# Weight conversions of the first layer issued later and in another order, a third pair of part buffers, earlier normalizations, and SBUF addresses moved by 32 bytes

## The chip, the core and the metric

The kernel runs on one core of a Trainium2 chip. The metric is the device time of one execution in microseconds (us). TensorE (PE) multiplies, VectorE (DVE) and ScalarE (ACT) do the elementwise work, SyncE (SP) and GpSimd (POOL) issue the transfers. Each engine runs its own instructions in order and waits on semaphores for the others.

## What is computed

Eight batches of eight heads attend to keys and values that are first averaged over groups of 8 rows; the result goes through two feed-forward layers of 512 to 2048 to 512.

```python
k_p = k.reshape(B, H, Sp, 8, D).mean(axis=3); v_p = v.reshape(B, H, Sp, 8, D).mean(axis=3)
scores = 1 / np.sqrt(D) * np.matmul(q, k_p.transpose(0, 1, 3, 2))
attn = softmax(scores); x = np.matmul(attn, v_p)      # 4608 tokens x 512
h = np.maximum(x @ w_in, 0.0);  x = h * h @ w_out      # layer 1, weights given as float64
h = x @ w2_in;  out = np.maximum(0.01 * h, h) @ w2_out # layer 2
```

## The kernel before

The 4608 tokens are nine blocks of 512. Float32 values are split into a high and a low part, so each product is three passes of 128x512 matmuls. A chunk is 128 of the 2048 hidden columns; there are 16, and a weight tile holds two of them.

**Weight conversion.** The weights of layer 1 arrive as pairs of 32-bit words and are converted in 16 tiles: numbers 0 to 7 are input weights, 8 to 15 output weights. `weight_steps` names the steps by letters: a is `exponent` on ACT (L231); b is `first_bits`, two DVE instructions (L235, L238); c is `low_term`, two DVE instructions (L249, L252); d is the sum on DVE (L293) and, in the same step, the copy of the high part on ACT (L296); e is the low part on DVE (L300), which reads that copy.

**First products of blocks 0 and 1** (`first_products`). The list `ORDER` has 32 units, each one call of `first`: 12 matmuls of one chunk (L872) into one of three accumulator banks, then `relu` on ACT (L882), then a store of the result to DRAM by POOL. Units 0 to 11 also carry the attention of block 1 (`second_attention`). A bank is used again three units later, after the relu that empties it. `conversion(u)` issues the weight steps of unit u; the table `begins` says at which unit tile n begins. In the unit of `begins` come a of the next tile and c, d of this one; in the unit behind it come b of the next tile and then e of this one. Tile 5 holds chunks 10 and 11 of block 0 (units 10 and 11), tile 6 chunks 12 and 13 (units 16 and 17), tile 7 chunks 14 and 15 (units 18 and 19).

**Second products of blocks 0 and 1** (`second_products`). 32 units again, one call of `second` each: 12 matmuls (L911). A unit first squares a stored result on ACT (L885) and splits the next one into `gh` and `gl` on DVE (`in_parts`, L890, L891; two buffers of each). Behind the matmuls come attention steps of block 2 (`Steps.upto`) and one step of the conversion of layer 2's weights (`w2.tick`). At the end of a block `finish` empties four banks, two on ACT (L927) and two on DVE (L925).

**The rest.** Blocks 2 to 8 run both products chunk by chunk with the next block's attention between; layer 2 follows, with 7 forms of a 2x2 scheme on 384 columns (L1299) and 512-column products (L1366). All orders are written out in Python; no scheduler moves anything.

**Addresses.** Pools on the left and the right side of SBUF hold all tiles. Before, a tile of 32 bytes (`pad`) stands at the end of the right side, and the tiles of attention and layer 1 and all weights begin at multiples of 64 bytes; the forms of layer 2 (`fh`, `fl`, `t1`, `t2`, `sums`) begin 32 bytes past one, by the tile `off`.

Of the kernel before, what the change touches and what calls it, by code (L numbers as in the profile page):

```python
# [16 lines left out]
P = 128  # L17
# [5 lines left out]

C_ID, C_PAR, C_VM, C_RA, C_RB, C_RP, C_N = 0, 128, 138, 140, 141, 142, 144

# [18 lines left out]
def attention_relu2_leaky_kernel(  # L44
# [36 lines left out]
    common = ctx.enter_context(tc.tile_pool(name="sb", bufs=1, side="left"))  # L81
    pad = ctx.enter_context(tc.tile_pool(name="pad", bufs=1, side="right"))
    nc.gpsimd.memset(pad.tile([P, 8], F32, tag="pad", name="pad"), 0.0)
    weights = ctx.enter_context(tc.tile_pool(name="wt", bufs=1, side="right"))
# [6 lines left out]
    BUFS = {"raw": 3, "val": 3, "qt": 2, "r": 3, "gh": 2, "gl": 2, "s": 2, "kt": 2, "kp": 2}  # L91
    BUFS.update({"m": 4, "l": 4, "st": 3, "val": 2})

# [24 lines left out]

    cst = sb([P, C_N], F32, "cst")
    ident = cst[:, C_ID : C_ID + P]  # L120
# [152 lines left out]
    def weight_steps(w, kind, i):  # L273


        st = {}

        def load_words():
            t = sb([P, 1024, 2], U32, weight_tag(kind, i))
            src, to = words_of(w, kind, i)  # L280
            nc.sync.dma_start(out=to(t), in_=src)
            st["low"], st["top"] = t[:, :, 0], t[:, :, 1]

        def bits():
            val = st["val"] = sb([P, 1024], U32, "val")
            first_bits(val, st["top"])

        def term():
            low_term(st["val"], st["top"], st["low"])

        def high():
            w = st["w"] = f32(st["val"])
            nc.vector.tensor_tensor(out=w, in0=w, in1=f32(st["low"]), op=ALU.add)  # L293
            t = st["parts"] = sb([P, 2, 1024], F32R, weight_tag(kind, i))
            place(kind, i, t)
            nc.scalar.copy(t[:, 0], w)  # L296

        def low():
            t = st["parts"]
            nc.vector.tensor_tensor(out=t[:, 1], in0=st["w"], in1=f32(t[:, 0]), op=ALU.subtract)  # L300

        return load_words, lambda: exponent(st["top"]), bits, term, high, low

    class Weights:
# [8 lines left out]
        def do(self, what, n):  # L313

            if n < len(self.steps):
                for x in what:
                    self.steps[n][" abcde".index(x)]()

# [106 lines left out]
    def k_mask(b):  # L425

        full, tail = KEYS // P, KEYS % P
        kp = kps.pop(b)
        km = (home() if b == 0 else sb([P, 512], F32, "r"))[:, : full * 2 * D]
        km = km.rearrange("p (c j d) -> p c j d", j=2, d=D)  # L430
        kt = sb([P, 2, D], F32, "km")
        par = cst[:, C_PAR : C_PAR + 2 * NK].rearrange("p (c j) -> p c j", j=2)
        for out, c0, c1, n in ((km, 0, full, P), (kt.unsqueeze(1), full, NK, tail)):
            shape = [n, c1 - c0, 2, D]
            nc.vector.tensor_tensor(
                out=out[:n],
                in0=kp[:n, c0:c1, :].unsqueeze(2).to_broadcast(shape),
                in1=par[:n, c0:c1, :].unsqueeze(3).to_broadcast(shape),
                op=ALU.mult,
            )  # L440
        kms[b] = km, kt
# [285 lines left out]
    def start():  # L727

        t0, rest = 0, {}
        for word in START:  # L730
# [18 lines left out]
            elif x in "abcde":  # L749
                w1.do(x, n)  # L750
            elif x == "k":
# [115 lines left out]
    def first(blk, c, at=None):  # L867
        hi, lo = xsplit[blk]
        ps = bank() if at is None else acc_bank(at % (KC - 1))
        for kc in range(KC):  # L870
# [15 lines left out]

    def in_parts(r):
        gh = sb([P, T], F32R, "gh")
        gl = sb([P, T], F32R, "gl")
        nc.vector.tensor_copy(gh, r)  # L890
        nc.vector.tensor_tensor(out=gl, in0=r, in1=f32(gh), op=ALU.subtract)  # L891
        return gh, gl
# [39 lines left out]
    class Steps:  # L932
# [8 lines left out]
        def upto(self, n):  # L941
            kind = "scores"
            while self.done < n:
                kind, step = self.steps[self.done]
                step()
                self.done += 1
            if kind != "scores" and self.done < len(self) and self.steps[self.done][0] == "normalize":
                self.steps[self.done][1]()
                self.done += 1
# [91 lines left out]

    begins = {2 * n - 2 if n < FC // 2 else FC - 2 + (n - FC // 2) * 5 // 2: n for n in range(1, FC - 1)}

    def conversion(u):
        if u in begins:
            n = begins[u]
            if n + 1 < FC - 1:
                w1.do("a", n + 1)
            w1.do("bcd" if n == 1 else "cd", n)
        elif u - 1 in begins:  # L1050
            n = begins[u - 1]
            if n + 1 < FC - 1:
                w1.do("b", n + 1)
            w1.do("e", n)

# [33 lines left out]
    def second_products():  # L1089
# [4 lines left out]
        for u in range(n_units):  # L1094
# [6 lines left out]
            if u + 1 < n_units:  # L1101
                g_next = in_parts(mids.pop(u + 1))
            if u >= n_units - 2:
                turn.pop(0)()
            second(c, acc, g)
            if 4 <= u < 9:
                w1.do("abcde"[u - 4], FC - 1)
            steps.upto(min(len(steps) * u // (n_units - 3), len(steps)))
            if u >= FC // 2:
                w2.tick()  # L1110
            if c == FC - 1:
# [366 lines left out]
```

## Time and profile before

| | us |
|---|---|
| median of 3 runs | 1737.35 |
| lowest, highest | 1734.87, 1738.37 |
| the profiled execution | 1736.26 |
| its span, first to last instruction | 1734.4 |
| PE busy in the span | 1693.5 |
| first products of blocks 0 and 1, from unit 0 | 47.1 to 170.6 |
| second products of blocks 0 and 1 | 170.6 to 280.9 |

The profiled execution lies 1.1 us under the median. Its span is 1.9 us shorter than its own time. The busy time of PE counts pipelined matmuls, so it does not tell the pace; the starts of neighbouring matmuls do.

### The profile page before, as it was taken

To read this page: it belongs to the slowest core of one execution; us is meant where nothing else is said; L and a number is where in the kernel's file an instruction comes from. 1 tells how busy PE (TensorE), PEld (TensorE's weight loads), DVE (VectorE), ACT (ScalarE), POOL (GpSimd) and SP (SyncE) were. 2 spreads that over 40 slices of the span, in tenths; PEclk is the share of its full clock that TensorE was granted. 3 is DMA by queue.
4 is the path that set the end of the run, shared out by engine and by line. 5 is a ranking of instruction groups with operands and counts; after the bars stand their busy time and mean duration, and the time that the engine had idled before them with its cause. 6 is when DMAs were issued, how large, how long until landed. Compare 5 with 4: busy or idle time off the path is not lost.

```text
span 1734.4 us, 21693 instructions
## 1 busy us (share of the span) xinstructions
PE 1693.5 (98%) x8312; PEld 1460.2 (84%) x8312; DVE 1110.3 (64%) x2020; ACT 627.1 (36%) x1496; POOL 19.1 (1%) x39
## 2 busy tenths in 40 slices
PE   6889999999999999999999999999999999999999
PEld 5768778888888888888888899999999999999997
DVE  7888777666666667565435555565566675666564
ACT  4555244344343443434333322332332332223221
POOL 0012000000000000000000000000000000000000
PEclk9999999999999999999999999999999999999999
DMA  8924552323222332231004202201202411320220
GB/s 229 338 72 145 174 182 89 92 92 95 88 95 88 104 104 73 95 112 61 13 25 162 81 1 73 74 12 61 74 25 98 170 48 62 110 103 13 104 74 37
DMA packets 106296, 162.44 MB, mean 94 GB/s; under 512 B 44112, under 2 KB 44240, under 8 KB 105168
## 3 DMA queue, kind: packets, MB, share of 16 engines
q1 hardware_dynamic: 103632, 152.67, 26.4%
q0 software_dynamic: 2560, 8.39, 1.3%
q8 instruction: 65, 1.06, 0.3%
q14 instruction: 39, 0.32, 0.1%
HBM read 111.75 MB, written 49.28 MB: 93 GB/s over the span
## 4 chain that ended last, share of the span: by engine, by line
PE 91%; DVE 6%; ACT 2%; issue 1%; DMA 0%; SPq 0%; DVEq 0%; ACTq 0%
PE acc L911 20%; PE ps L1299 20%; PE ps L872 18%; PE acc L1366 15%; PE ps L1366 8%; PE acc L872 4%; PE ps L587 2%; PE ps L650 1%; PE ps L551 1%; PE ps L702 0%; ACT s L608 0%; PE ps L701 0%; PE ps L704 0%; PE ps L703 0%; DVE xl L679 0%
## 5 line engine op out<-in xcount | busy, mean ns | idle before, releaser
L911 PE MATMUL acc<-gh,wo 128*128 128x512 f32 x1152 | 296.4, 395 | 4.0 <-DVE gh L890 1.9
L872 PE MATMUL ps<-xh,wi 128*128 128x512 f32 x896 | 297.0, 394 | 0.0
L1299 PE MATMUL ps<-fh,wi 128*128 128x384 f32 x1344 | 289.2, 337 | 0.1
L1299 PEld LDWEIGHTS ps<-fh,wi 128*128 128x128 f32 x1344 | 243.1, 188 | 22.1 <-DVE gh L1312 0.4
L911 PEld LDWEIGHTS acc<-gh,wo 128*128 128x128 f32 x1152 | 213.1, 188 | 51.1 <-DVE gh L890 4.5
L1366 PE MATMUL acc<-wo,sh 128*128 128x512 f32 x768 | 205.6, 390 | 0.0
L872 PEld LDWEIGHTS ps<-xh,wi 128*128 128x128 f32 x896 | 168.2, 188 | 35.0 <-issue 0.2
L872 PE MATMUL ps<-xl,wi 128*128 128x512 f32 x448 | 174.5, 389 | 0.0
L1299 PE MATMUL ps<-fl,wi 128*128 128x384 f32 x672 | 171.2, 336 | 0.0
L890 DVE CAST gh<-r 128x512 fp32r<-128x512 f32 x112 | 47.7, 425 | 187.0 <-ACT r L885 186.7
L911 PE MATMUL acc<-gl,wo 128*128 128x512 f32 x576 | 159.6, 391 | 0.0
L1366 PEld LDWEIGHTS acc<-wo,sh 128*128 128x128 f32 x768 | 141.5, 188 | 15.6
L882 ACT ACTIVATE r<-ps 128x512 f32<-128x512 f32 x112 | 67.7, 605 | 212.0 <-PE ps L872 212.0
L911 PEld LDWEIGHTS acc<-gl,wo 128*128 128x128 f32 x576 | 108.7, 189 | 23.4
L1299 PEld LDWEIGHTS ps<-fl,wi 128*128 128x128 f32 x672 | 121.4, 188 | 0.0
L1366 PE MATMUL acc<-wo,sl 128*128 128x512 f32 x384 | 120.2, 392 | 0.0
L608 ACT ACTIVATE s<-ps,m 128x72 f32<-128x72 f32 x240 | 72.3, 331 | 105.9 <-DVE m L599 105.9
L1312 DVE TENSOR_TENSOR u<-gh,ps 128x384 f32<-128x384 f32 x48 | 26.6, 554 | 120.0 <-PE ps L1299 120.0
L1366 PE MATMUL ps<-wo,sh 128*128 128x512 f32 x384 | 102.8, 389 | 0.0
L872 PEld LDWEIGHTS ps<-xl,wi 128*128 128x128 f32 x448 | 84.2, 188 | 16.6
L1366 PEld LDWEIGHTS acc<-wo,sl 128*128 128x128 f32 x384 | 72.1, 188 | 18.3 <-DVE sl L1347 3.7
L891 DVE TENSOR_TENSOR gl<-r,gh 128x512 fp32r<-128x512 f32 x112 | 77.6, 692 | 8.0 <-DVE gh L890 0.9
(206 smaller groups left out, 2362.2 us busy)
## 6 DMA issues: line engine op xcount, KB each, us to landing
wi<-in_moe_w_in SPq DMA_DIRECT2D x8, 1024.0 KB
wo<-in_moe_w_out SPq DMA_DIRECT2D x8, 1024.0 KB
val<-in_moe_w_in SPq DMA_DIRECT2D x16, 512.0 KB
val<-in_moe_w_out SPq DMA_DIRECT2D x16, 512.0 KB
w2p<-val SPq DMA_DIRECT2D x16, 512.0 KB
wo<-w2p SPq DMA_DIRECT2D x8, 1024.0 KB
xh<-x SPq DMA_DIRECT2D x10, 768.0 KB
xl<-x SPq DMA_DIRECT2D x10, 768.0 KB
```

Of the source, the lines that this page charges most:

```text
L551: nc.tensor.transpose(ps[:, cc * P : (cc + 1) * P], raw[:, cc * P : (cc + 1) * P], ident)
L587: nc.tensor.matmul(ps[: r0 + n, c2 * PAIR : (c2 + 1) * PAIR], lhsT=qt[:, cc, : r0 + n], rhs=kts[b][:, keys], start=True, stop=True,)
L608: nc.scalar.activation(out=s[:, g, :], in_=ps[:, h * SP : (h + 1) * SP], func=AF.Exp, bias=m[:, g : g + 1], accum_out=None if i in early e ...
L650: nc.tensor.transpose(ps[:, cc * P : (cc + 1) * P], flat[:, cc * PAIR : cc * PAIR + P], ident)
L872: nc.tensor.matmul(ps, lhsT=w[:, kc], rhs=x[kc], start=(kc == 0 and n == 0), stop=(kc == KC - 1 and n == 2),)
L882: nc.scalar.activation(out=r, in_=ps, func=AF.Relu)
L890: nc.vector.tensor_copy(gh, r)
L891: nc.vector.tensor_tensor(out=gl, in0=r, in1=f32(gh), op=ALU.subtract)
L911: nc.tensor.matmul(acc[m], lhsT=w[:, m * P : (m + 1) * P], rhs=x, start=(c == 0 and n == 0), stop=(c == FC - 1 and n == 2),)
L1299: nc.tensor.matmul(at, lhsT=w[:, FORMS[j], kc], rhs=x[j][:, kc], start=m == 0 and j in (0, 1, 4), stop=m == 5, skip_group_check=True,)
L1312: nc.vector.tensor_tensor(out=out_, in0=x, in1=at, op=ALU.add)
L1366: nc.tensor.matmul(self.acc[i], lhsT=x[g % 2][c][t][:, at], rhs=self.outs[p][:, part_, c], start=p == 0 and m == 0, stop=p == PAIRS - 1 an ...
```

## The change

Five things are done. The ACT copy of the high part becomes a step of its own, D; it still directly follows d, except for tile 1, where it moves to the next unit. In the second unit of a tile, e now stands ahead of b of the next tile. Tiles from number 6 on begin at unit 2n + 1 (13, 15, ... 29) where tile 6 began at 10, tile 7 at 12, tile 8 at 14 and the later ones about every 2.5 units up to 29; a and b of tile 6 stand in unit 12. The accumulator of unit u is bank (u + 2) mod 3 and not u mod 3. In the second products every third pair of parts goes into two `st` buffers; the last two units of block 0 carry no attention steps and no tick; and a normalization may be taken ahead of one pooling step. All tiles move by 32 bytes, except the identity, the pooled keys `kt`, and the small `m` and `l`, which stay at multiples of 64; the forms of layer 2 come to multiples of 64.

```diff
-C_ID, C_PAR, C_VM, C_RA, C_RB, C_RP, C_N = 0, 128, 138, 140, 141, 142, 144
+C_ID, C_PAR, C_VM, C_RA, C_RB, C_RP, C_N = 16, 0, 10, 12, 13, 14, 144
...
-    pad = ctx.enter_context(tc.tile_pool(name="pad", bufs=1, side="right"))
-    nc.gpsimd.memset(pad.tile([P, 8], F32, tag="pad", name="pad"), 0.0)
...
-    BUFS.update({"m": 4, "l": 4, "st": 3, "val": 2})
+    BUFS.update({"m": 4, "l": 3, "st": 3, "val": 2})
...
-    cst = sb([P, C_N], F32, "cst")
+    cst = sb([P, C_N + 8], F32, "cst")[:, :C_N]
...
             place(kind, i, t)
-            nc.scalar.copy(t[:, 0], w)
+
+        def high_copy():
+            nc.scalar.copy(st["parts"][:, 0], st["w"])
...
-        kt = sb([P, 2, D], F32, "km")
+        kt = sb([P, 2 * D + 8], F32, "km")[:, : 2 * D].rearrange("p (j d) -> p j d", j=2)
...
-        ps = bank() if at is None else acc_bank(at % (KC - 1))
+        ps = bank() if at is None else acc_bank((at + 2) % (KC - 1))
...
-    def in_parts(r):
-        gh = sb([P, T], F32R, "gh")
-        gl = sb([P, T], F32R, "gl")
+    def in_parts(r, tags=("gh", "gl")):
+        gh, gl = (sb([P, T], F32R, tag) for tag in tags)
...
         def upto(self, n):
-            kind = "scores"
+            kind = ""
...
-            if kind != "scores" and self.done < len(self) and self.steps[self.done][0] == "normalize":
-                self.steps[self.done][1]()
+            near = "".join(k[:1] or "-" for k, _ in self.steps[self.done : self.done + 2])
+            if kind != "scores" and near.lstrip("-")[:1] == "n":
+                step = self.steps.pop(self.done + near.index("n"))
+                self.steps.insert(self.done, step)
+                step[1]()
...
-    begins = {2 * n - 2 if n < FC // 2 else FC - 2 + (n - FC // 2) * 5 // 2: n for n in range(1, FC - 1)}
+    LATE = 6
+    begins = {2 * n - 2 if n < LATE else 2 * n + 1: n for n in range(1, FC - 1)}
...
-            if n + 1 < FC - 1:
+            if n + 1 < FC - 1 and n + 1 != LATE:
                 w1.do("a", n + 1)
-            w1.do("bcd" if n == 1 else "cd", n)
+            w1.do("bcd" if n == 1 else "cdD", n)
...
-            if n + 1 < FC - 1:
+            w1.do("De" if n == 1 else "e", n)
+            if n + 1 < FC - 1 and n + 1 != LATE:
                 w1.do("b", n + 1)
-            w1.do("e", n)
+        elif u == 2 * LATE:
+            w1.do("ab", LATE)
...
-                g_next = in_parts(mids.pop(u + 1))
+                apart = (u + 1) % 3 == 2 and u + 3 < n_units
+                g_next = in_parts(mids.pop(u + 1), ("st", "st") if apart else ("gh", "gl"))
...
-            steps.upto(min(len(steps) * u // (n_units - 3), len(steps)))
-            if u >= FC // 2:
-                w2.tick()
+            if c < FC - 2 or blk:
+                steps.upto(min(len(steps) * u // (n_units - 3), len(steps)))
+                if u >= FC // 2:
+                    w2.tick()
```

On DVE, behind unit 11, the conversions stand back to back. Before, from b of tile 7 on (`wi_719` is tile 7 as loaded, `wi_983` the parts of tile 6, `wo_852` tile 8, `wi_1057` the parts of tile 7):

```order
L235 TENSOR_SCALAR val<-wi_719 128x1024 [waits DMAHW7_49]
L238 SCALAR_TENSOR_TENSOR val<-wi_719,val 128x1024 [waits DVE_49]
L300 TENSOR_TENSOR wi_983<-val,wi_983 128x1024
L249 TENSOR_SCALAR wi_719<-val 128x1024 [waits DVE_49]
L252 SCALAR_TENSOR_TENSOR wi_719<-wi_719 128x1024 [waits DVE_49]
L293 TENSOR_TENSOR val<-val,wi_719 128x1024 [waits DVE_49]
L235 TENSOR_SCALAR val<-wo_852 128x1024 [waits DMAHW0_49,Activation_49]
L238 SCALAR_TENSOR_TENSOR val<-wo_852,val 128x1024 [waits DVE_49]
L300 TENSOR_TENSOR wi_1057<-val,wi_1057 128x1024 [waits Activation_49]
```

Now, at the same place (`wi_611` is tile 6 as loaded, `wi_1058` its parts, `wi_714` tile 7, `wi_1102` its parts):

```order
L233 TENSOR_SCALAR val<-wi_611 128x1024 [waits DMAHW6_49,Activation_49]
L236 SCALAR_TENSOR_TENSOR val<-wi_611,val 128x1024 [waits DVE_49]
L247 TENSOR_SCALAR wi_611<-val 128x1024 [waits DVE_49]
L250 SCALAR_TENSOR_TENSOR wi_611<-wi_611 128x1024 [waits DVE_49]
L291 TENSOR_TENSOR val<-val,wi_611 128x1024 [waits DVE_49]
L300 TENSOR_TENSOR wi_1058<-val,wi_1058 128x1024 [waits Activation_49]
L233 TENSOR_SCALAR val<-wi_714 128x1024 [waits DMAHW7_49]
L236 SCALAR_TENSOR_TENSOR val<-wi_714,val 128x1024 [waits DVE_49]
L247 TENSOR_SCALAR wi_714<-val 128x1024 [waits DVE_49]
L250 SCALAR_TENSOR_TENSOR wi_714<-wi_714 128x1024 [waits DVE_49]
L291 TENSOR_TENSOR val<-val,wi_714 128x1024 [waits DVE_49]
L300 TENSOR_TENSOR wi_1102<-val,wi_1102 128x1024 [waits Activation_49]
```

Tile 6 now stands here whole, and e of a tile (L300) directly follows its d (L291), where b of the next tile stood between.

On ACT at units 11 to 14, now (`acc_1003` is unit 11's accumulator, `acc_1021` unit 12's, `acc_1041` unit 13's, `wi_1058` the parts of tile 6):

```order
L882 ACTIVATE r<-acc_1003 128x512 [waits DMASW0_49,PE_49,Activation_49]
L229 ACTIVATE wi_611<-wi_611 128x1024 [waits DMAHW6_49]
L882 ACTIVATE r<-acc_1021 128x512 [waits DMASW1_49,PE_49,Activation_49]
L229 ACTIVATE wi_714<-wi_714 128x1024 [waits DMAHW7_49]
L296 CAST wi_1058<-val 128x1024 [waits DVE_49]
L882 ACTIVATE r<-acc_1041 128x512 [waits DMASW2_49,PE_49,Activation_49]
L882 ACTIVATE r<-acc_1065 128x512 [waits DMASW3_49,PE_49,Activation_49]
```

The exponent step of tile 6 (L229) has come from unit 8 to behind the relu of unit 11, and the relu of unit 13 stands behind the copy of tile 6.

On DVE at the end of block 0 in the second products, before, the copies of `finish` (L925) stand behind the steps of a tick (L252, L353):

```order
L252 SCALAR_TENSOR_TENSOR val<-val 128x512
L890 CAST gh<-xh 128x512
L891 TENSOR_TENSOR gl<-xh,gh 128x512
L353 TENSOR_TENSOR r<-r,val 128x512
L925 COPY r<-acc_1456 128x512
L925 COPY r<-acc_1458 128x512
```

On DVE at the same place, now (`acc_1451` and `acc_1453` are banks 1 and 3 of block 0):

```order
L889 CAST gh<-xl 128x512
L890 TENSOR_TENSOR gl<-xl,gh 128x512
L889 CAST gh<-xh 128x512
L890 TENSOR_TENSOR gl<-xh,gh 128x512
L924 COPY r<-acc_1451 128x512
L924 COPY r<-acc_1453 128x512
```

Only parts stand ahead of the copies; the tick and the transposed probabilities have moved behind them.

## Rows read from the trace of the kernel before

**Rows 1.** The page's first part: engine, busy us, share of the span, instructions

```profile
PE 1693.5 (98%) x8312; PEld 1460.2 (84%) x8312; DVE 1110.3 (64%) x2020; ACT 627.1 (36%) x1496; POOL 19.1 (1%) x39
```

**Rows 2.** Waits of PE over the whole span: us in total, times, longest us

```profile
PE acc L872 <- DVE wi L300: 5.0, 2, 4.7
...
PE acc L911 <- DVE gh L890: 1.9, 5, 0.6
...
PE acc L872 <- ACT wi L296: 1.6, 1, 1.6
...
PE acc L911 <- DVE r L925: 1.3, 1, 1.3
```

**Rows 3.** Timeline of PE at unit 10: start us, us, instruction, idle before

```profile
104.42 1.22 PE L872 MATMUL acc<-xh,wi 128*128 128x512 f32 x2 [4.71 <-DVE wi L300]
```

**Rows 4.** Timeline of PE: first matmul of unit 11, of the second products

```profile
113.43 0.39 PE L872 MATMUL acc<-xh,wi 128*128 128x512 f32 x1
...
116.20 0.39 PE L872 MATMUL acc<-wo,wi 128*128 128x512 f32 x1
...
170.60 0.61 PE L911 MATMUL acc<-gh,wo 128*128 128x512 f32 x2
```

**Rows 5.** Timeline of DVE ahead of unit 10's wait

```profile
101.29 0.68 DVE L235 TENSOR_SCALAR val<-wi 128x1024 uint32<-128x1024 uint32 x1
...
103.15 1.22 DVE L300 TENSOR_TENSOR wi<-val,wi 128x1024 fp32r<-128x1024 f32 x1
```

**Rows 6.** Groups of DVE instructions, 44 to 175 us: busy, mean ns, idle before

```profile
L619 DVE TENSOR_REDUCE l<-s 128x8 f32<-128x576 f32 x4 | 3.0, 751 | 1.4 <-ACT s L608 1.4
```

**Rows 7.** Busy us of PE, PEld, DVE, ACT, POOL, clock, DMA, units 11 to 31

```profile
113.40:170.60 57.20, 57.20 (x254) 47.32 (x253) 52.06 (x54) 28.56 (x40) 11.07 (x20) 1.00 0.33 113
```

**Rows 8.** Timeline of DVE: the last conversions ahead of the second products

```profile
157.74 0.68 DVE L235 TENSOR_SCALAR val<-wo 128x1024 uint32<-128x1024 uint32 x1
...
159.60 1.22 DVE L300 TENSOR_TENSOR wo<-val,wo 128x1024 fp32r<-128x1024 f32 x1
160.74 0.69 DVE L249 TENSOR_SCALAR wo<-val 128x1024 uint32<-128x1024 uint32 x1
...
162.72 1.23 DVE L293 TENSOR_TENSOR val<-val,wo 128x1024 f32<-128x1024 f32 x1
165.06 1.22 DVE L300 TENSOR_TENSOR wo<-val,wo 128x1024 fp32r<-128x1024 f32 x1 [1.11 <-ACT wo L296]
```

**Rows 9.** Timeline of ACT: relu of unit 11, an exponent, a copy, three squares

```profile
116.45 0.60 ACT L882 ACTIVATE r<-acc 128x512 f32<-128x512 f32 x1 [2.28 <-PE acc L872]
116.94 1.14 ACT L231 ACTIVATE wo<-wo 128x1024 f32<-128x1024 f32 x1
...
163.98 1.05 ACT L296 CAST wo<-val 128x1024 fp32r<-128x1024 f32 x1 [0.69 <-DVE val L293]
...
168.62 1.66 ACT L885 ACTIVATE xh<-xh 128x512 f32<-128x512 f32 x3
```

**Rows 10.** Busy us of the engines, then the granted clock, around unit 10

```profile
100.50:107.40 6.90, 2.98 (x7) 2.40 (x8) 6.72 (x9) 1.60 (x5) 0.46 (x1) 0.51 0.22 78
```

**Rows 11.** Timeline of PE: units 16 and 17 of the second products

```profile
220.93 0.70 PE L911 MATMUL acc<-gh,wo 128*128 128x512 f32 x2 [0.56 <-ACT xh L885]
222.89 2.50 PE L911 MATMUL acc<-gh,wo 128*128 128x512 f32 x6 [1.25 <-DVE r L925]
...
226.87 2.00 PE L911 MATMUL acc<-gh,wo 128*128 128x512 f32 x8
```

**Rows 12.** Timeline of PE in layer 2

```profile
1204.80 0.51 PE L1299 MATMUL ps<-fl,wi 128*128 128x384 f32 x2
1205.15 1.07 PE L1366 MATMUL ps<-wo,sh 128*128 128x512 f32 x4
```

**Rows 13.** ACT's copies to `fh` (L1206) by source: ns min, median, max

```profile
L1206 ACT CAST fh<-xl x30: 830/833/838, 1030.1 to 1663.1; 128x768 fp32r<-128x768 f32 x30
L1206 ACT CAST fh<-t x22: 821/836/838, 929.8 to 1657.0; 128x768 fp32r<-128x768 f32 x22
```

More of the change, by code (lines that the diff above doesn't have):

```diff
@@ L300, in low @@
             nc.vector.tensor_tensor(out=t[:, 1], in0=st["w"], in1=f32(t[:, 0]), op=ALU.subtract)
-        return load_words, lambda: exponent(st["top"]), bits, term, high, low
+        return load_words, lambda: exponent(st["top"]), bits, term, high, low, high_copy
     class Weights:
@@ L316, in do @@
                 for x in what:
-                    self.steps[n][" abcde".index(x)]()
+                    self.steps[n][" abcdeD".index(x)]()
     class Stored:
@@ L749, in start @@
             elif x in "abcde":
-                w1.do(x, n)
+                w1.do("dD" if x == "d" else x, n)
             elif x == "k":
@@ L1106, in second_products @@
             if 4 <= u < 9:
-                w1.do("abcde"[u - 4], FC - 1)
-            steps.upto(min(len(steps) * u // (n_units - 3), len(steps)))
-            if u >= FC // 2:
-                w2.tick()
+                w1.do(("a", "b", "c", "dD", "e")[u - 4], FC - 1)
+            if c < FC - 2 or blk:
+                steps.upto(min(len(steps) * u // (n_units - 3), len(steps)))
+                if u >= FC // 2:
+                    w2.tick()
             if c == FC - 1:
```

## The prediction

> **What bounds the kernel now.** I read the page's engine shares first: PE is busy for nearly the whole span [rows 1], so a change can only win where PE waits, and loses wherever it makes PE wait. The waits of PE come next [rows 2]: what concerns this change is the low part of an input weight (L300, 5.0 us, one wait of 4.7), its high part (L296, 1.6), the parts of the squares (L890, 1.9) and the copy that empties a bank (L925, 1.3). All lie in the first 281 us. Then I follow three places in the timelines.
>
> The first is unit 10: PE stands 4.71 us for e of tile 5 [rows 3], and DVE comes to that e at 103.15, directly behind b of tile 6 [rows 5].
>
> The second is the stretch from unit 11 to the second products, 113.43 to 170.60 [rows 4]. There PE is the bound: 57.20 of 57.20 us busy [rows 7], and 20 units from 116.20 to 170.60 make 2.72 us a unit [rows 4]. But DVE has little to spare: 52.06 us busy in the same 57.2 [rows 7].
>
> The third is the end of block 0 in the second products, where unit 16's matmuls are stretched by a wait for L925 [rows 2, 11].
>
> **The change, part by part.** The sum is made against the profiled execution, 1736.26 us, which stands 1.1 us under the median of 1737.35.
>
> *Units 0 to 11.* b of tile 6 goes from the DVE path ahead of e of tile 5: 103.15 - 101.29 = 1.86 us [rows 5]. In the units before, e ahead of b lets PE start a unit earlier, and the exponentials with it; DVE waited 1.4 us for these in four normalizations [rows 6], of which I take 1.0, an estimate. The new bank order lets unit 0 start without waiting for the pooled keys, but the units behind it wait for DVE's conversions, so that is in the 1.0 already. Together -2.9 us. The bounds are -1.9 (b alone) and -6.6 (both weight waits of [rows 2], 5.0 + 1.6).
>
> *Units 12 to 31.* Here the change adds a wait, and this is the term that decides. Call X the start of unit 11. The exponent a of tile 6 now stands on ACT behind the relu of unit 11. That relu began 3.02 us behind X and the next ACT instruction 3.51 behind it (116.45 and 116.94 against 113.43 [rows 4, 9]); an exponent takes 1.14 [rows 9]. So b of tile 6 starts on DVE at X + 4.7, and from there DVE has nine whole tiles (6 to 14) ahead of the first pair of parts, and nothing else.
>
> What a tile costs is read at the last tiles of before: b takes 159.60 - 157.74 = 1.86 us, e takes 160.74 - 159.60 = 1.14, c takes 162.72 - 160.74 = 1.98 [rows 8]. From d to e it depends on what stands between. The copy of the high part (1.05 us [rows 9]) can only start when d has ended, and e reads it. Before, b of the next tile fills that time. Only for the last tile there is no next b, and there the row shows it: DVE idles 1.11 us for L296, and d to e is 165.06 - 162.72 = 2.34 [rows 8]. In the new order e directly follows d for every tile. DVE works strictly in order, so b of the next tile, though ready, is queued behind the waiting e. A tile is then 1.86 + 1.98 + 2.34 + 1.14 = 7.32 us, while PE needs 2 x 2.72 = 5.44 for the two units that carry it. Who waits for that: the relu of a tile's first unit stands on ACT behind the copy, a bank comes free with its relu, and PE needs the bank three units later. The lead of a few us is used up after about three tiles, and from then on PE goes at DVE's 7.32.
>
> The ninth e starts at X + 4.7 + 9 x 7.32 - 1.14 = X + 69.4, and the ninth copy has just ended on ACT. Behind it ACT has two relus (0.49 each from start to start, as 116.45 to 116.94), three squares (1.66) and the relu of unit 31 (0.60) [rows 9]. By (u + 2) mod 3 unit 31 holds bank 0, which the second products write first, so they begin at X + 69.4 + 1.0 + 1.7 + 0.6 = X + 72.7. Before it was 170.60 - 113.43 = 57.2. This part is +15.5 us. If the bank were no hindrance the first parts would, a good 1.3 earlier. Bounds: +13 (that, and 7.2 a tile) and +17 (another 0.15 a tile for semaphores).
>
> *The clock at the start of the second products.* Units 30 and 31 can run once the relu of unit 27 is done, behind the eighth copy at X + 62.1, and end about X + 68.2; PE then stands for some 4.5 us. When it stood 4.71 us at unit 10 the granted clock was 0.51, the lower of its two levels, from 100.50 to 107.40 [rows 3, 10], which is 2.98 us after the matmuls resumed. At half pace that loses 1.5 us. I add +1.5 (0 to 3).
>
> *The end of block 0.* Ahead of L925 there is no tick any more, so a bank is copied as soon as its last matmul is done, under the matmuls of the next bank. Unit 16 took 226.87 - 220.93 = 5.94 us for 12 matmuls, which take 2.72, and it had waited 0.56 before [rows 11]: 3.8 us, with the slower clock that followed (six matmuls in 2.50 [rows 11]). Of this I give back 1.0, an estimate: the postponed steps put DVE work of about 3 us ahead of the parts of unit 18 or so. So -2.8 (0 to -3.8).
>
> *The third pair* lets DVE split ahead of PE's reads. But where PE waited longest for parts [rows 2], DVE came to them late by the pooling and the conversion that stand ahead of them, and the change leaves these there. I take 0 (to -1.9). *Normalizations ahead of pooling* reach into blocks 2 to 8; no wait of PE for a normalization stands among [rows 2]'s larger ones. I take 0 (-1 to +1).
>
> *Addresses.* In the kernel before, all weights start at multiples of 64 bytes, so no row shows a weight load 32 bytes on. The nearest rows: ACT's copies to `fh` take 833 ns from a source at a multiple of 64 and 836 from one at 32 bytes past [rows 13]; matmuls with the moving operand `fl` at 32 past take (1205.15 - 1204.80) / 2 = 0.175 us for 384 columns [rows 12], those of layer 1 with all operands at 0 take 2.72 / 12 = 0.227 for 512 [rows 4]. The difference, 0.052 for 128 columns, leaves about 17 ns that is not columns in either. A start 32 bytes on changed nothing there, so I take 0. The bounds are wide: those 17 ns over the 7,200 three-pass matmuls of both layers (3,456 and 3,744) would be 120 us either way; with the rows beside it I leave that to the chances.
>
> DVE's instructions with one tensor and constants are quick: b's first takes 0.68 us where d, on two tensors of the same length, takes 1.23 [rows 8]. No row shows such an instruction at 32 past; were its pace lost there, two of them a tile over nine tiles would add 18 x 0.55 = 9.9 us. [...]
>
> **Sum.** -2.9 + 15.5 + 1.5 - 2.8 = +11.3 us. That makes 1747.6 for the profiled execution and 1748.7 for the median.
>
> **The rivals.** *The copy stays hidden.* If e did not idle, a tile would be 7.32 - 1.11 = 6.2 us, nine of them 55.9, and the ninth e would end at X + 60.6; the second products would start some 4 us late and not 15.5, without the clock's loss. With -2.9 and -2.8 the time is 1735.7, no change. For it: DVE has nine tiles in 57 us, which just fits. Against it: the 1.11 in [rows 8], which has the very order that all tiles now have. It decides as soon as the idle is under 0.3 us. Chance 0.05.
>
> *The addresses pay.* The other side of my forecast: a weight load 32 bytes on is cheaper for every matmul. To be faster than before by over 0.2%, it has to win 11.3 + 3.5 = 14.8 us, 2.1 ns of each of 7,200 matmuls; at 3 ns the time is 1748.7 - 21.6 = 1727. For it only that nothing excludes it, against it [rows 12, 13]. Chance 0.06; 0.05 for the same loss, 1770.
>
> *The small gains are large and the cost small.* All low ends at once: -6.6 + 13 + 0 - 3.8 - 1.9 - 1 = -0.3, 1737. Some way towards it, 1739, chance 0.05.
>
> *The clock stays low for longer.* From unit 18 on PE idles about 1.9 us in every two units, and 0.56 + 1.25 us were enough for a drop at unit 16 [rows 11]. Two units with such a drop take 5.44 + 1.7, still under 7.32, so it is paid only at the end: +3, 1752. It is in the range.
>
> **How the numbers follow.** Forecast 0.79, hidden copy 0.05, addresses 0.06 and 0.05, small cost 0.05. A measurement of this kernel tells 0.2% (3.5 us) from no change. Slower: 0.79 + 0.05 = 0.84. Same: 0.05 + 0.04 = 0.09. Faster: 0.06 + 0.01 = 0.07. The range goes from 1741 (an early gain of 5, a cost of 14 in units 12 to 31, no clock loss, block 0's 3.8 and the third pair's 1.9 whole: -5 + 14 - 3.8 - 1.9 = +3.3) to 1757 (all high ends: -1.9 + 17 + 3 + 0 + 1 = +19.1); the hidden copy, the small cost and the addresses are left out of it.
>
> **What would show it.** Right: in the trace after, DVE idles about 1.1 us for L296 before each L300 from tile 6 to 14; units from about 18 on come in pairs 7.3 us apart; the second products start 72 to 73 us after unit 11; the wait of unit 10 is still there, about 3 to 4 us, and comes 3 us earlier; there is no wait for the copy of `finish`. Wrong: units 12 to 31 at 2.72 us throughout, or a distance other than 0.227 us between neighbouring 512-column matmuls in layer 2, which would be the addresses.

## The result, and the profile after

The changed kernel takes 1750.24 us (median of 4 runs, 1748.98 to 1752.06) against 1737.22 (4 runs of the kernel before, 1734.87 to 1738.37): ratio 1.0077, 95% interval 1.0060 to 1.0095. The forecast was 1748.7. The profiled execution took 1748.98 with a span of 1746.9, 12.5 more than the span before.

Where the 12.5 us lie is read from the starts of the first matmuls of each stage in the two traces (us from the span's start):

| start of | before | after | stretch that ends there, longer by |
|---|---|---|---|
| unit 0 of the first products | 47.08 | 44.97 | -2.11 |
| unit 11 | 113.43 | 110.28 | -1.04 |
| second products | 170.60 | 184.49 | +17.04 |
| block 2 | 280.86 | 292.19 | -2.56 |
| block 8 | 897.96 | 910.25 | +0.96 |
| layer 2 | 985.00 | 997.28 | -0.01 |
| last matmul | 1730.28 | 1742.78 | +0.22 |

The stretch from unit 11 to the second products loses more than the whole difference; those ahead of it and behind it win. The page's first part of after, to be read against [rows 1]:

```profile
PE 1697.1 (97%) x8312; PEld 1462.8 (84%) x8312; DVE 1112.5 (64%) x2020; ACT 626.0 (36%) x1496; POOL 18.7 (1%) x38
```

As many instructions as before on PE, DVE and ACT (POOL has one less), 3.6 us more of PE, 2.2 more of DVE: the engines' shares say nothing on the loss. The losing stage does, in the busy times of the engines (columns as in [rows 7]):

```profile
110.25:184.45 74.20, 61.15 (x253) 47.66 (x252) 59.17 (x59) 31.54 (x44) 11.19 (x20) 0.98 0.24 86
```

PE was busy for all of its 57.2 us there [rows 7]; now 13 of 74 are idle. PE's waits in this stage of after (us in total, times, longest):

```profile
PE acc L872 <- ACT xh L882: 3.6, 2, 1.8
PE acc L872 <- ACT xl L882: 3.6, 2, 1.8
PE acc L872 <- ACT r L882: 3.2, 2, 1.8
PE acc L910 <- DVE gh L889: 2.7, 1, 2.7
```

PE waits for relus, six times, 1.5 to 1.8 us each: for a bank. That is a symptom. Why the relu is late stands on ACT, and why ACT is late on DVE. The first two tiles behind unit 11 on DVE in after, the last e and the first part:

```profile
114.94 0.69 DVE L233 TENSOR_SCALAR val<-wi 128x1024 uint32<-128x1024 uint32 x1 [3.27 <-ACT wi L229]
115.67 1.23 DVE L236 SCALAR_TENSOR_TENSOR val<-wi,val 128x1024 uint32<-128x1024 uint32 x1
116.93 0.70 DVE L247 TENSOR_SCALAR wi<-val 128x1024 uint32<-128x1024 uint32 x1
...
118.92 1.23 DVE L291 TENSOR_TENSOR val<-val,wi 128x1024 f32<-128x1024 f32 x1
121.26 1.23 DVE L300 TENSOR_TENSOR wi<-val,wi 128x1024 fp32r<-128x1024 f32 x1 [1.12 <-ACT wi L296]
122.40 0.76 DVE L233 TENSOR_SCALAR val<-wi 128x1024 uint32<-128x1024 uint32 x1
...
128.79 1.23 DVE L300 TENSOR_TENSOR wi<-val,wi 128x1024 fp32r<-128x1024 f32 x1 [1.12 <-ACT wi L296]
...
181.45 1.23 DVE L300 TENSOR_TENSOR wo<-val,wo 128x1024 fp32r<-128x1024 f32 x1 [1.12 <-ACT wo L296]
182.94 0.43 DVE L889 CAST gh<-xh 128x512 fp32r<-128x512 f32 x1 [0.27 <-ACT xh L885]
```

The bracket on L300 is what [rows 8] showed once and what now stands in every one of nine tiles: DVE idles 1.1 us for the copy, with the next tile's b ready behind it. The distance from L300 to L300 is 7.53 us (121.26, 128.79). ACT at the same time, around the second copy of that stretch and around the last:

```profile
127.70 1.05 ACT L296 CAST wi<-val 128x1024 fp32r<-128x1024 f32 x1 [4.45 <-DVE val L291]
128.66 1.08 ACT L882 ACTIVATE r<-acc 128x512 f32<-128x512 f32 x2
...
180.36 1.05 ACT L296 CAST wo<-val 128x1024 fp32r<-128x1024 f32 x1 [5.50 <-DVE val L291]
181.32 1.08 ACT L882 ACTIVATE xl<-acc 128x512 f32<-128x512 f32 x2
182.28 1.67 ACT L885 ACTIVATE xh<-xh 128x512 f32<-128x512 f32 x3
183.84 0.59 ACT L882 ACTIVATE xl<-acc 128x512 f32<-128x512 f32 x1
```

ACT is idle for 4.4 to 5.5 us (2.5 ahead of the first copy), then makes the copy, and only then the relus behind it (at 128.66 those of units 15 and 16, whose matmuls ended at 124.1 and 126.8): it too is in order. From unit 18 on the units come in pairs; unit 20 starts at 136.82, unit 22 at 144.34, 7.52 later. PE in after (where the stretch begins, one of its stops, and the start of the second products):

```profile
110.28 0.39 PE L872 MATMUL acc<-xh,wi 128*128 128x512 f32 x1
...
144.34 0.50 PE L872 MATMUL acc<-wo,wi 128*128 128x512 f32 x1 [1.76 <-ACT r L882]
...
184.49 1.88 PE L910 MATMUL acc<-gh,wo 128*128 128x512 f32 x7 [2.69 <-DVE gh L889]
```

The last bracket names a wrong releaser: that part was ready at 182.94 + 0.43 = 183.37, while the relu of unit 31 ends at 183.84 + 0.59 = 184.43, 0.06 before PE goes on.

### The profile page after: what moved, and what is told of

The parts are those of the page before. It is cut to its first block, busy times and chain, and to the rows that moved or that the text cites. A ratio compares the mean times of both kernels' runs of the same rounds, so it can differ in the third digit from the quotient of the medians.

```text
span 1746.9 us, 21674 instructions
## 1 busy us (share of the span) xinstructions
PE 1697.1 (97%) x8312; PEld 1462.8 (84%) x8312; DVE 1112.5 (64%) x2020; ACT 626.0 (36%) x1496; POOL 18.7 (1%) x38
## 4 chain that ended last, share of the span: by engine, by line
PE 86%; DVE 10%; ACT 2%; issue 1%; DMA 0%; SPq 0%; DVEq 0%; ACTq 0%
PE ps L1306 20%; PE acc L910 19%; PE ps L872 17%; PE acc L1373 15%; PE ps L1373 7%; PE ps L587 2%; PE acc L872 1%; DVE val L291 1%; DVE val L236 1%; PE ps L650 1%; PE ps L551 1%; ACT s L608 1%; DVE wo L250 0%; DVE wi L250 0%; DVE xl L679 0%
## 5 line engine op out<-in xcount | busy, mean ns | idle before, releaser
L910 PE MATMUL acc<-gh,wo 128*128 128x512 f32 x1072 | 275.0, 395 | 4.4 <-DVE gh L889 4.4
L910 PEld LDWEIGHTS acc<-gh,wo 128*128 128x128 f32 x1072 | 198.9, 188 | 46.3 <-DVE gh L889 3.2
L910 PE MATMUL acc<-gl,wo 128*128 128x512 f32 x536 | 148.6, 391 | 0.0
L910 PEld LDWEIGHTS acc<-gl,wo 128*128 128x128 f32 x536 | 101.1, 189 | 21.4
```

The costliest lines, as they stand in the source:

```text
L910: nc.tensor.matmul(acc[m], lhsT=w[:, m * P : (m + 1) * P], rhs=x, start=(c == 0 and n == 0), stop=(c == FC - 1 and n == 2),)
```

## The experiments

All times that follow are medians of 10 runs (9 for the last kernel); beside each group stands the kernel before on the same chip, 30 or 31 runs: 1737.07 for e1 to e4, 1736.61 for e5 to e8, 1737.38 for e9 to e12.

### What makes the tiles slow: order, late begin, or both

Edit of e1:

```diff
             n = begins[u - 1]
+            if n >= LATE and n + 1 < FC - 1:
+                w1.do("b", n + 1)
+                w1.do("e", n)
+                return
```

> The changed kernel with one edit: from tile 6 on, b of the next tile stands ahead of e of this tile again, as in the kernel before; the table of begins stays late. Theory (DVE idles for the copy of the high part in every tile): the idle of 1.1 us ahead of L300 goes for tiles 6 to 13 and stays for tile 14; a tile takes 6.1 to 6.2 us on DVE where it takes 7.52 in the changed kernel; the last e starts about 61 us behind unit 11 (71.2 in the changed kernel) and the second products about 64 behind it (74.2); the time is 10 to 11 us under the changed kernel's, about 1739.7 (1738 to 1742). First rival (it is the late begin alone, DVE has too little time in whatever order): second products still 72 to 74 behind unit 11, 1750. Second rival (the new SBUF addresses slow the conversions or the matmuls): 1748 to 1750 as well, with a tile at 7.5 us though no idle is left.

Edit of e2:

```diff
-    begins = {2 * n - 2 if n < LATE else 2 * n + 1: n for n in range(1, FC - 1)}
+    begins = {2 * n - 2 if n < FC // 2 else FC - 2 + (n - FC // 2) * 5 // 2: n for n in range(1, FC - 1)}
...
-            if n + 1 < FC - 1 and n + 1 != LATE:
+            if n + 1 < FC - 1:
...
-        elif u == 2 * LATE:
-            w1.do("ab", LATE)
```

> The changed kernel with one edit: the table of begins of the kernel before (tile 6 at unit 10, tile 7 at 12, tile 8 at 14 ...); e still stands directly behind d and its copy, ahead of b of the next tile. Theory (both the idle for the copy and the late begin cost): a tile still takes 7.5 us, but tile 6 is finished about 2.5 us behind unit 11 and seven tiles fewer than nine are left behind tile 7, so the last e starts 61 to 62 us behind unit 11 and the second products 64 to 65 behind it; about 9.7 us under the changed kernel, 1740.5 (1739 to 1743). Rival (the late begin alone): second products 57 to 58 behind unit 11, 1733 to 1734. Rival (the order alone): second products 72 to 74 behind it, 1750.

e3 has both edits.

> The changed kernel with both edits: begins of the kernel before, and from tile 6 on b of the next tile ahead of e; up to tile 5 e stays ahead of b. Theory: units 12 to 31 go at 2.72 us again, the second products start 57 to 58 us behind unit 11, and what is left of the change is its gains, about 3 us up to unit 11 and 2.5 us in the second products, less 1 in blocks 2 to 8: 1732 to 1734 against 1737.2 before, 17 under the changed kernel. The gain of this run over the changed kernel is less than the sum of the two single edits' gains, since PE's own pace of 2.72 a unit is the floor. Rival (the other edits cost something too, the addresses above all): 1737 or more.

| | e ahead of b (copy exposed) | b ahead of e (copy hidden) |
|---|---|---|
| begins late | after: 1750.24; 74.21 | e1: 1738.42; 63.14 |
| begins as before | e2: 1739.19; 64.46 | e3: 1733.99; 58.06 |

The second number is the distance from unit 11 to the second products; before it was 57.17. The intervals of the ratio to before are 0.9999 to 1.0018 (e1), 1.0001 to 1.0021 (e2) and 0.9974 to 0.9993 (e3). Either edit alone takes away 10 to 11 us of the 17 and both together 16, since PE's own pace, 2.72 us a unit, is the floor below. None of the single-cause rivals holds: the loss is the idle for the copy in every tile, made worse by DVE having nine whole tiles left at unit 11. DVE in e1, from d of tile 6 on:

```profile
119.87 1.23 DVE L291 TENSOR_TENSOR val<-val,wi 128x1024 f32<-128x1024 f32 x1
121.01 0.69 DVE L233 TENSOR_SCALAR val<-wi 128x1024 uint32<-128x1024 uint32 x1
121.73 1.23 DVE L236 SCALAR_TENSOR_TENSOR val<-wi,val 128x1024 uint32<-128x1024 uint32 x1
122.88 1.22 DVE L300 TENSOR_TENSOR wi<-val,wi 128x1024 fp32r<-128x1024 f32 x1
...
129.03 1.22 DVE L300 TENSOR_TENSOR wi<-val,wi 128x1024 fp32r<-128x1024 f32 x1
```

No bracket on L300, and 6.15 us from one to the next: 1.4 less than in after, for the same work.

### The second products of blocks 0 and 1

e4 is the kernel before with the condition `if c < FC - 2 or blk:` around the steps and the tick, e6 the kernel before with the third pair.

> The kernel before with one edit: the last two units of block 0 in the second products carry no attention steps and no tick, so the copies that empty the banks stand ahead of them. Theory (this edit alone brings what the second products of blocks 0 and 1 gained, 110.3 to 107.7 us): the wait of 1.25 us in unit 16 and the slower clock behind it go, second products 107.5 to 108.5 us long, time 1734.5 to 1735.5, 2 to 2.8 under before. Rival (the third pair of part buffers brings it, or the clock at unit 0): second products 109.5 to 110.3, 1736.5 to 1737.2.

> The kernel before with one edit: every third pair of parts in the second products of blocks 0 and 1 goes into two st buffers. The second products took 110.3 us before, 108.4 with the edit at the end of block 0 alone, 107.7 in the changed kernel. Theory (the third pair brings the 0.7 that are left): 109.3 to 109.8 us for the second products, time 1736.3 to 1736.8. Rival one (nothing, as predicted: the parts come late by what stands ahead of them on DVE): 110.1 to 110.5, 1737. Rival two (it removes the wait at unit 16 too): 108 to 108.7, 1735.3.

e4 took 1736.19 (ratio 0.9988 to 1.0007, with 1 inside), e6 1737.26 (0.9995 to 1.0014). Their times tell little, but the stages in their traces, one execution each, do (us between first matmuls of second products; "slow" is the number of neighbouring 512-column matmuls 0.43 us apart at unit 16, where others are 0.227):

| | units 0-3 | 4-14 | 15-17 | 18 to block 2 | slow |
|---|---|---|---|---|---|
| before | 11.96 | 34.81 | 13.14 | 50.36 | 8 |
| e6, third pair | 11.93 | 34.76 | 13.15 | 50.32 | 7 |
| e7, addresses | 11.97 | 34.81 | 11.55 | 50.26 | 0 |
| e8, normalizations | 11.95 | 34.79 | 11.55 | 50.36 | 0 |
| e4, end of block 0 | 11.97 | 33.79 | 10.99 | 51.67 | 0 |
| after | 11.48 | 33.71 | 10.91 | 51.60 | 0 |

The third pair alone does nothing (rival one). The edit at the end of block 0 brings most of the stretch's gain in these traces (108.4 us from unit 0 to block 2, as its theory had), but its median of 1736.19 lies above the theory's 1734.5 to 1735.5. It takes 1.0 out of units 4 to 14 (PE's own attention work, 216.35 to 217.37 in the trace before, which now comes later), 2.15 out of units 15 to 17, and gives 1.3 back behind. e4 at the place of [rows 11], without a wait:

```profile
219.21 1.98 PE L911 MATMUL acc<-gh,wo 128*128 128x512 f32 x8
221.02 1.07 PE L911 MATMUL acc<-gl,wo 128*128 128x512 f32 x4
```

e7 and e8 leave this place as it was and still took 11.55, since no matmuls at half pace followed the wait in them. At the same place in e8:

```profile
223.39 0.70 PE L911 MATMUL acc<-gh,wo 128*128 128x512 f32 x2 [0.56 <-ACT xh L885]
225.34 1.66 PE L911 MATMUL acc<-gh,wo 128*128 128x512 f32 x6 [1.26 <-DVE r L925]
```

The waits are those of [rows 11], the six matmuls take 1.66 and not 2.50. So the edit is worth 1.85 us against an execution with the slow stretch and 0.2 against one without.

### The early gain

e5 is the kernel before with `acc_bank((at + 2) % (KC - 1))`.

> The kernel before with one edit: unit u of the first products writes bank (u + 2) mod 3. In the four kernels measured so far that have it unit 0 starts at 43.97 to 46.09 us, without it at 47.08 and 46.84. Theory (this edit alone makes unit 0 start 1 to 3 us earlier, since it need not wait for the bank of the pooled keys, and part of that reaches unit 11): unit 0 at 44.5 to 46, unit 11 at 111.5 to 113, time 1735 to 1736.5. Rival (the units behind wait for the weight conversions on DVE anyway, so the early start is used up): unit 0 early, unit 11 at 113.0 to 113.6, time 1736.5 to 1737.5.

e9 is e3 with the copy of tile 1 back in unit 0, e10 is e3 with the old bank order:

```diff
-            w1.do("bcd" if n == 1 else "cdD", n)
+            w1.do("bcdD" if n == 1 else "cdD", n)
...
-            w1.do("De" if n == 1 else "e", n)
+            w1.do("e", n)
```

> e3_both_undone with one more edit undone: the copy of tile 1's high part (D, on ACT) stands directly behind d in unit 0 again, and not in unit 1 behind the relu and the copy of the queries. In all kernels with the old place unit 2 began 57.3 to 59.2 us into the span (also with the new bank order alone), in those with the new place at 53.5 to 55.6. Theory (the early gain comes from this copy: before it stood on ACT ahead of the queries' copy L556, for which PE waits): unit 2 at 56.5 to 58.5, unit 11 at 111.5 to 113.0, time 1735.5 to 1737. Rival (the early gain comes from e ahead of b, as the prediction had it): unit 2 at 54 to 55, unit 11 at 109.5 to 110.5, time 1734.

> e3_both_undone with the bank order of the kernel before (unit u in bank u mod 3). Theory (the new bank order costs 0.9 us at the end of unit 31, since the second products write bank 0 first and must wait for its relu, and gives 0.45 back in their first units; ahead of unit 2 it is worth 1 us or more now that the copy of tile 1 is out of the way): second products 57.2 behind unit 11 (58.1 in e3), their first four units 11.96 us (11.52 in e3), unit 2 at 54.5 to 56, time 1734 to 1735.5. Rival (the bank order alone carries the early gain once the copy is late): unit 2 at 57 or later, 1736 or more. Rival (it is worth nothing ahead of unit 2): unit 2 at 53.5 to 54, time 1733.5.

The span's start varies by some 2 us against the work, so the units are counted here from the last attention step of block 0 on DVE (L679 ahead of unit 0; in e5 it is this row):

```profile
46.55 0.69 DVE L679 TENSOR_TENSOR xl<-ps,xh 128x512 fp32r<-128x512 f32 x1 [0.24 <-ACT xh L678]
```

| from there, us | unit 0 | unit 2 | unit 8 | unit 10 | e of tile 5 | unit 11 |
|---|---|---|---|---|---|---|
| before | 1.43 | 12.15 | 44.79 | 53.33 | 57.50 | 67.79 |
| e5: new bank order alone | -0.82 | 12.14 | 44.82 | 53.33 | 57.50 | 68.28 |
| e9: with e ahead of b, tile 1's copy early | -0.82 | 13.49 | 46.22 | 54.17 | 56.53 | 67.00 |
| e10: with e ahead of b, copy late, old banks | 1.43 | 12.39 | 45.68 | 53.66 | 56.01 | 67.42 |
| e3: all three | -0.82 | 8.72 | 43.98 | 51.98 | 54.29 | 64.75 |
| after | -0.82 | 8.71 | 44.00 | 50.97 | 54.22 | 64.49 |

The times are 1738.20 for e5 (1.0001 to 1.0020), 1736.62 for e9 (0.9986 to 1.0005), 1734.15 for e10 (0.9974 to 0.9992). The bank order alone starts unit 0 2.25 us earlier and unit 2 no earlier: on this point e5's rival holds. But e5 is 1.6 us slower than before, outside both ranges; its trace shows 0.45 of that at the second products (the last relu, below), and 0.5 at unit 11, where three more matmuls ran at half pace than in before; the rest is open. With the late copy the bank order counts at unit 2, which comes 3.4 us earlier than before. The late copy without it comes to 12.39, of which 1.4 us are seven matmuls of unit 0 at half pace in this execution (0.43 and not 0.227 us apart), so about 11.0 by an estimate; e10's theory missed unit 2 (59.48) by that and by a late start, and its median fits. ACT and PE of e9 between units 1 and 2 show why the copy matters:

```profile
54.21 1.04 ACT L296 CAST wi<-val 128x1024 fp32r<-128x1024 f32 x1 [2.84 <-DVE val L291]
55.16 0.59 ACT L882 ACTIVATE r<-acc 128x512 f32<-128x512 f32 x1
55.65 0.58 ACT L556 COPY qt<-ps 128x512 f32<-128x512 f32 x1
```

```profile
56.28 1.65 PE L587 MATMUL acc<-kt,qt 128*128 128x144 f32 x8 [3.17 <-ACT qt L556]
```

The copy waits for d, the queries' copy L556 is queued behind it on ACT, and PE stands for that. With the copy late, ACT in after:

```profile
50.25 0.59 ACT L882 ACTIVATE r<-acc 128x512 f32<-128x512 f32 x1
50.73 0.59 ACT L556 COPY qt<-ps 128x512 f32<-128x512 f32 x1
53.22 1.04 ACT L296 CAST wi<-val 128x1024 fp32r<-128x1024 f32 x1 [1.91 <-DVE val L291]
```

The place of the copy is worth 2.25 us at unit 11 (67.00 in e9, 64.75 in e3), and as much in the medians, each against its own before (-0.8 and -3.1). That is e9's theory, though unit 2 (60.27) and unit 11 (113.78) came later in the span than it had them. The bank order isn't told from none by the medians of e10 and e3 (-3.2 and -3.1).

### Addresses and normalizations

> The kernel before with the SBUF addresses of the changed kernel and nothing else (all tiles 32 bytes on, but for the identity, the pooled keys and the small tiles; the forms of layer 2 at multiples of 64). Theory (the address makes no difference to matmuls, weight loads, copies or conversions): neighbouring 512-column matmuls stay 0.227 us apart, 384-column ones 0.175, the last product of layer 1 and the end keep their distance of 750 us to within 0.3, first instruction of a b step 0.68 us; time 1736.5 to 1737.7. Rival (a start 32 bytes on costs or saves a nanosecond or more at each of 7,200 matmuls): 1744 and over or 1730 and under.

> The kernel before with one edit: a normalization may be taken ahead of one pooling step. From the first product of block 2 to that of block 8 the kernels measured so far took between 0.7 us less and 1.0 us more than before, with the edit (four kernels) and without it (one, 0.8 more). Theory (the edit neither gains nor loses, those are differences from execution to execution): 616.4 to 618.1 us for this stretch (617.1 before), time 1736.3 to 1738. Rival (the edit costs): 618.5 or more, 1738.5. Rival (it pays): under 616, 1736.

e7: 1735.74, ratio 0.9984 to 1.0003. Layer 2 and a conversion in e7:

```profile
1202.93 0.51 PE L1297 MATMUL ps<-fl,wi 128*128 128x384 f32 x2
1203.28 1.07 PE L1364 MATMUL ps<-wo,sh 128*128 128x512 f32 x4
```

```profile
127.68 0.69 DVE L233 TENSOR_SCALAR val<-wo 128x1024 uint32<-128x1024 uint32 x1
128.40 1.22 DVE L236 SCALAR_TENSOR_TENSOR val<-wo,val 128x1024 uint32<-128x1024 uint32 x1
129.55 1.22 DVE L298 TENSOR_TENSOR wo<-val,wo 128x1024 fp32r<-128x1024 f32 x1
130.68 0.70 DVE L247 TENSOR_SCALAR wo<-val 128x1024 uint32<-128x1024 uint32 x1
```

(1203.28 - 1202.93) / 2 = 0.175 us, as in [rows 12]; 0.69 us for the first instruction of b, where [rows 8] have 0.68. From layer 2 to the last matmul e7 takes 745.33 us, before 745.28. No effect of the addresses can be seen; the median lies below the 1736.5 to 1737.7 expected, with 1 inside the interval.

e8: 1736.81, 0.9991 to 1.0010. Blocks 2 to 7 take 616.86 us in it, 617.11 before. Over all kernels of this study the stretch takes 616.3 to 618.1, with the edit (616.4 to 618.1) as without it (616.3 to 617.9). The +0.96 of after is within that.

### A version that is faster than both

e3 is already faster than the kernel before. Two further edits: `acc_bank((at + 2 * (at < 12)) % (KC - 1))` (e11), and on top of it, in unit 9, e of tile 5 ahead of the split of the pooled values, with d of tile 6 in unit 11 (e12).

> e3_both_undone with the new bank order up to unit 11 and that of the kernel before from unit 12 on, so unit 31 is in bank 1 again. Theory: second products 57.2 behind unit 11 and not 58.1, first four units 11.96 and not 11.52, so 0.4 us are won: 1733.5 (1732.5 to 1734.5), with unit 2 as in e3. Rival (the wait at the start of the second products is for the parts, not for the relu of unit 31): 58.1 again, 1734.

> e11_bank_switch with the low part of tile 5 (e, for which unit 10 waits) on DVE ahead of the split of the pooled values in place of behind it, and d of tile 6 behind the attention's last steps of unit 11 in place of ahead of them. Theory (unit 10's wait is for what stands ahead of e on DVE, and nothing else is late): the wait of 2.85 us for L300 in unit 10 shrinks to about 1.0, unit 11 comes 1 to 2 us earlier, 1.1 us of it are given back by d behind unit 11: time 1732.5 (1731.5 to 1734). Rival (the attention steps behind unit 10 are bound by DVE and come at the same time, so the wait only moves): unit 11 as in e3, about 65.6 us behind unit 0, time 1734 to 1735.

e11: 1733.21, ratio 0.9966 to 0.9986; second products 57.17 behind unit 11 (58.06 in e3) and 11.97 us for their first four units (11.52). So the relu of unit 31 in bank 0 costs 0.9 and gives 0.45 back, as expected.

e12: 1732.21, with the same interval as e11: not told apart. In its trace unit 11 starts at 64.91 in the count above, in e11's at 64.82, which looks like the rival. But the two executions differ already ahead of the edit. Behind the same stop ahead of unit 5, six of the unit's matmuls ran at half pace in e12 and none in e11. First e11, then e12:

```profile
71.38 1.16 PE L381 MATMUL ps<-st,cst 128*128 128x128 f32 x8 [1.97 <-ACT s L608]
72.84 0.63 PE L872 MATMUL acc<-xh,wi 128*128 128x512 f32 x2
```

```profile
70.80 1.35 PE L381 MATMUL ps<-st,cst 128*128 128x128 f32 x8 [1.97 <-ACT s L608]
72.80 1.05 PE L872 MATMUL acc<-xh,wi 128*128 128x512 f32 x2
```

So e12 begins unit 10 1.55 us later (53.57 against 52.02), and makes it up: from unit 10 to unit 11 it takes 11.34 us, e11 12.81. PE of e12 in unit 10 and behind it:

```profile
100.58 0.73 PE L872 MATMUL acc<-xh,wi 128*128 128x512 f32 x2 [0.98 <-DVE wi L300]
...
106.98 0.47 PE L703 MATMUL ps<-ptl,v_hi 128*128 128x448 f32 x1 [2.05 <-DVE ptl L669]
```

The wait for L300 fell from 2.85 to 0.98. PE then stands at L703, for a DVE step queued behind c of tile 6; still, 1.47 us of the gain arrive at unit 11, within the theory's 1 to 2. Of these 0.88 are given back behind unit 11 (58.05 us to the second products, 57.17 in e11), where the theory had 1.1. The traces thus favour the theory, with some 0.6 us won, an estimate from one execution of each; the medians don't settle it.

## Why the prediction was right, step by step

*Units 12 to 31 (+15.5 forecast, +17.04 measured).* The mechanism is the one named, shown by the brackets on L300 and by e1 to e3. b of tile 6 starts 4.66 us behind unit 11 (forecast 4.7), the idle is 1.11 to 1.12 (1.11), the last e starts 71.17 behind (69.4), PE goes on 3.04 later (3.3). What was mis-sized is the tile: 7.52 and not 7.32. The forecast took it from a place where e stands between b and c. Then the next instruction starts 1.14 behind the second one of b; now c follows, which reads b's result, and starts 1.26 behind it (115.67 to 116.93). That goes with the reading: in both traces the same holds for d behind c, which it reads (1.26), and for e or b behind an instruction that they don't read (1.13 to 1.15). And the first instruction of b, behind e, takes 0.76 in these tiles and not 0.68; behind the same e in units 1 to 9 of after it takes 0.68 to 0.69, so why is open. 0.2 us for eight tiles are 1.6 of the missing 1.8. The 0.15 us a tile for semaphores behind the bound of +17 stand in no run: from d's end (118.92 + 1.23 = 120.15) to the start of the copy on ACT (120.18) pass 0.03 us, and from the copy's end (120.18 + 1.05 = 121.23) to e (121.26) 0.03 again.

*The clock at the start of the second products (+1.5 forecast, 0 measured).* This step failed. PE stood 2.69 us there, not 4.5, and went on at a granted clock of 1.00. Windows of after (columns as in [rows 10]): in unit 30, during that stop, behind it:

```profile
174.40:178.60 4.20, 4.17 (x13) 3.32 (x14) 4.10 (x5) 0.47 (x1) 1.10 (x2) 0.68 0.35 129
181.80:184.45 2.65, 0.00 (x0) 0.00 (x0) 2.33 (x4) 2.65 (x7) 1.12 (x2) 1.00 0.34 125
184.45:190.00 5.55, 5.51 (x24) 4.59 (x25) 3.37 (x6) 1.66 (x3) 0.54 (x1) 1.00 0.84 298
```

The slow stretch came earlier, in units 30 and 31 (eight matmuls 0.41 to 0.43 us apart, not 0.227; clock 0.50 from 176.0 to 179.0), where DVE was the bound and it cost nothing. It also used up most of the time by which PE stood less than forecast. In e1 it came where it was forecast, behind a stop of 2.89 us: twelve matmuls at half pace, 2.4 us, and the first four units took 14.35 and not 11.5.

```profile
174.35:178.60 4.25, 4.22 (x10) 3.35 (x11) 2.06 (x4) 1.64 (x3) 0.78 (x1) 0.50 0.66 215
```

*Units 0 to 11 (-2.9 forecast; -3.15 in the profiles, -3.3 in the count above).* The size is right. PE's wait in unit 10 is still 3.8 (forecast 3 to 4). e of tile 5 comes 3.28 earlier: 1.86 for b, as taken, and 1.42 for what stands earlier, where 1.0 was taken. But the forecast gave this rest to the exponentials and did not cost the move of tile 1's copy at all, though the diff shows it. DVE's wait for the exponentials did fall, from 1.4 us [rows 6] to 0.3, but in e9, with the copy early, it is still 0.9. e9 and e3 put 2.25 us on that copy, and e9, with e ahead of b but the copy early, reaches unit 11 only 0.8 us earlier than before. So that the size came out is in part luck. By unit 8 only 0.8 of the 3.4 us at unit 2 are left, which is the forecast's reason why an early unit 0 is worth little.

*The end of block 0 (-2.8 forecast; -2.1 for the second products behind unit 3).* 3.2 are gone and 1.3 given back, where 3.8 and 1.0 were taken; the other 0.2 of after came on top of e4's. The waits of [rows 2] for L925 are gone. Most of the gain, 1.6, is the slow stretch of [rows 11], which some executions of the old order don't have. That the forecast came near is in part luck of the execution that it was read from.

*Third pair, normalizations, addresses (0 forecast).* e6, e8 and e7 show each alone at no measurable effect. For the quick DVE instructions the sum took 0 where the prediction's bound was 9.9 us, and no run had shown that 0; e7 does. At 32 bytes past a multiple of 64 the first instruction of b takes 0.69 us and the first of c 0.70, where [rows 8] have 0.68 and 0.69. One slip had no part in the sum: by the prediction's own figures 0.227 - 4 x 0.052 leaves, as an estimate, 19 ns of a matmul that is not columns, and not 17, so its bound for the addresses would have been 137 us and not 120.

Summed, the stages gave -3.15 + 17.04 - 2.56 + 0.96 + 0.2 = +12.5 against +11.3. Too little for the tile (1.8) stood against too much for the clock (1.5), so part of the closeness is luck. A term for the bank order at the start of the second products, +0.9 and -0.45 (e11), was seen only as the wait for the last relu and is small.

## What to carry to other kernels

Where a step on one engine reads a copy that another engine makes of the step before, put independent work between them: a tile takes 7.52 us on DVE without it (after) and 6.15 with it (e1). The one place in the old trace where nothing stood between (the last tile) gave the price of every tile in the new order, to within 3%. A move of one instruction on an engine that is busy for only 36% of the span (ACT, [rows 1]) can matter more than the edits with large names, as the copy of tile 1 did with 2.25 us: what counts is what is queued behind it. And two traces are to be compared from a place just ahead of the edit: counted from ahead of unit 0, e12 seems to win nothing, because a slow stretch in unit 5, which the edit doesn't touch, hid what was won behind unit 10.

## What the runs showed of the hardware that was not expected

The clock's answer to the same stop differs between executions: after waits of 0.56 and 1.25 us at unit 16 the granted clock fell to the lower of the two levels in these traces (0.50, as from 101.0 to 107.0 in before, and 1.00, as from 107.5 to 113.4) in three kernels (before, e5, e6: 7 or 8 matmuls at 0.43 us, where others are at 0.227; a mean of 0.57 from 222.90 to 226.90 in before) and not in two others (e7, e8: 1.00 from 225.30 to 228.00 in e8). After 1.97 us ahead of unit 5 six matmuls ran at half pace in e12 and none in e11. Of six stops of 1.5 to 1.8 us from unit 20 to unit 30 of after, only the last was followed by such matmuls. After 2.69 us it stayed at 1.00 in after, after 2.89 us it was 0.50 in e1. What decides it no run here settles. Behind the stop of unit 10, up to which before, e4, e6 and e8 have the same order of instructions, 5, 7, 6 and 8 matmuls ran at half pace: 0.6 us from execution to execution.
